# A smaller first mix, pooled outputs summed in PSUM, and the second phase in five chunks, in a kernel of attention, channel mix and gated convolution

## The chip, the cores and the metric

The kernel runs on one core of a Trainium2 chip. The metric is device time in microseconds (us) of one execution; three executions of the kernel before took 561.58, 561.82 and 563.68 us, a median of 561.82. TensorE (PE) multiplies, VectorE (DVE) and ScalarE (ACT) work elementwise, GpSimd (POOL) does small fills, and SyncE (SP) issues most of the DMA transfers. Each engine works through its own instructions in the order in which they were written; semaphores hold an instruction back until what it needs is there.

## The reference

Three layers follow each other. Layer 1, for 4 batches, 8 heads, 576 tokens and 64 channels a head, is the sum of an attention over tokens averaged in fours (repeated four times) and a local attention over the tokens nearer than 4. Its output has T = 2304 rows of 512 channels. Layer 2 mixes each row with the one before it, and layer 3 is a gated convolution.

```python
out_d = sm_attn(q_d, k_d, v_d)                  # means of 4 tokens
out_up = np.repeat(out_d, factor, axis=2)
mask = np.abs(pos[:, None] - pos[None, :]) < factor
...
x = out_up + out_local
...
xk = mu_k * x + (1.0 - mu_k) * x_prev
xr = mu_r * x + (1.0 - mu_r) * x_prev
k = np.maximum(xk @ w_k, 0.0)                   # 512 -> 1024
v = k * k @ w_v                                 # 1024 -> 512
r = 1.0 / (1.0 + np.exp(-(xr @ w_r)))           # 512 -> 512
x = r * v
...
h = np.maximum(x @ w_in, 0.0)                   # 512 -> 1024
conv_out += conv_w[k][None, None, :] * hp[:, k:k + S, :]   # 3 taps
gate = 1.0 / (1.0 + np.exp(-conv_out))
return h * gate @ w_out                         # 1024 -> 512
```

## The kernel before, in words

All of it is one program of steps. Every step names its engine, what it reads and what it writes; a long table of numbers (ORDER, line 24) gives the order in which the steps are emitted, and a second one (SECOND) says, where two engines could do a step, which does it. The order of each engine's instructions is thereby fixed by hand; nothing is reordered later. Channels lie on the partitions and tokens along the columns.

Phase one is the attention and the first matrix products (w_k and w_v). Attention goes by batch, by groups of four heads (two groups a batch) and by blocks of 32 tokens (18 blocks). For a group there are pooled keys and queries (a DVE sum of fours, line 511), local scores (PE, lines 540 and 549), their softmax on DVE and ACT, pooled scores (line 614), transposes (690, 741), pooled outputs (709, copied to the tile od by ACT, 721) and local outputs (760). A DVE add (775) sums the two into the tile xT. The matrix products are done by chunks of tokens (`chunks_`, line 258): 288, 288 and then 432 at a time. The first chunk is special: batch 0 is attended in two parts, blocks 0 to 9 and blocks 10 to 17 (`half`, line 432), and the first 288 tokens go through `first_mix` (line 851) while the second part and batch 1 are still being attended. There the weights arrive through three buffers st_d; two ACT instructions (382, 401) and one DVE instruction (385) turn each 512 KB tile into f32, and PE multiplies by the f32 tile as it stands, up (862) and down (892). The same tile is then split into a high part (ACT or DVE, 421/423) and a low part (DVE, 427) of a rounded type. All later chunks use three products of these parts (`mix`, line 916, with lines 926 and 976). Ten steps of idle products (`fills`, line 1032) keep PE occupied at the start.

The pooled values of batch 0 are made by PE from the value tile vw (`fold`, line 484). So the first output of a head group waits for its vw transfer.

Phase two goes over T in six chunks of 384 outputs (CH, line 247), each computed on 386 columns, as the convolution needs one neighbour on each side. For each chunk: `load_chunk` (1175) reads x back from DRAM and mixes rows, `gate` (1252) makes r and x1 (line 1259: 4 tiles of 12 products), `hidden` (1292) makes h (line 1303: 8 tiles of 12 products), the three taps (1348, 1349, 1352) and the gate, and `outp` (1375) multiplies by w_out, 24 products of 512 columns for 128 tokens (line 1383), one chunk late beside the next one. Here the two edge columns of each chunk are computed twice, once in either chunk.

## Time and profile before

| what | value |
|---|---|
| median of three runs | 561.82 us |
| the profiled execution's own time | 561.85 us |
| its span, first to last instruction | 560.0 us |
| PE busy | 545.9 us, 97% |
| DVE busy | 370.1 us, 66% |
| ACT busy | 306.6 us, 55% |
| mean granted TensorE clock | 0.990 |

The span is 1.85 us shorter than the profiled execution's time. Busy time is the share in which at least one instruction of the engine runs. The chain of waits follows the work that ended last back to its start; it names, for each stretch of time, the engine and line that the end hung on. The granted clock is the share of TensorE's full rate.

### The profile page before, as it was taken

The page shows a single profiled execution, that of the slowest core. Times are in us where ns is not written, and L with a number is a line of the kernel's source. Part 1 is how long each engine was busy: PE and PEld are TensorE (multiplying, and loading weights), DVE is VectorE, ACT ScalarE, POOL GpSimd, SP SyncE. Part 2 cuts the span into 40 slices and gives each one's busy share as a digit, 9 for nine tenths or more (in the row PEclk, how much of TensorE's full clock was granted, in tenths as well). Part 3 has the DMA queues.
Part 4 walks back from the last instruction along what each step waited for, and adds up shares of the span by engine and source line. Part 5 has one row for each costly group of instructions (what it writes and reads, how often), then busy time and mean ns, then how long its engine had stood idle before and what let it go on. Part 6 is the DMA issues. An engine that isn't in the chain of part 4 may idle for free.

```text
span 560.0 us, 12998 instructions
## 1 busy us (share of the span) xinstructions
PE 545.9 (97%) x5412; PEld 495.1 (88%) x5412; DVE 370.1 (66%) x720; ACT 306.6 (55%) x716; POOL 29.5 (5%) x132
## 2 busy tenths in 40 slices
PE   6899989999999999999999999999999999999996
PEld 3677769999999999999999998898998998999985
DVE  5778777677566646563374897487667676677750
ACT  4678956736553656554575555454545355444431
POOL 5001010110101000000000000000000000000000
PEclk9979998999999999999999999999999999999999
DMA  8658767647643503722127400402200130001002
GB/s 345 224 181 261 242 204 265 197 122 237 180 184 89 198 2 134 259 94 95 66 70 253 135 2 0 151 1 76 75 1 38 58 96 19 1 0 39 10 29 94
DMA packets 26395, 66.19 MB, mean 118 GB/s; under 512 B 2656, under 2 KB 12384, under 8 KB 25312
## 3 DMA queue, kind: packets, MB, share of 16 engines
q1 hardware_dynamic: 24608, 62.41, 31.7%
q0 software_dynamic: 1728, 2.95, 3.3%
q8 instruction: 42, 0.69, 0.5%
q14 instruction: 17, 0.14, 0.1%
HBM read 51.20 MB, written 14.16 MB: 117 GB/s over the span
## 4 chain that ended last, share of the span: by engine, by line
PE 93%; DMA 2%; DVE 2%; ACT 1%; issue 1%; SPq 0%; ACTq 0%; DVEq 0%
PE a L1383 18%; PE mm L926 16%; PE mm L976 16%; PE mm L1303 9%; PE a L1303 8%; PE a L1259 4%; PE mm L1259 4%; PE mm L862 3%; PE a L760 3%; PE mm L892 3%; DMA vw<-in_vw 2%; PE a L709 2%; PE a L549 2%; PE a L741 2%; PE a L690 1%; PE a L614 1%
## 5 line engine op out<-in xcount | busy, mean ns | idle before, releaser
L1383 PE MATMUL a<-wk,wv 128*128 128x512 f32 x432 | 101.0, 390 | 0.1
L1383 PEld LDWEIGHTS a<-wk,wv 128*128 128x128 f32 x432 | 80.9, 188 | 16.4 <-ACT xT L1398 0.4
L926 PE MATMUL mm<-xk,wk 128*128 128x432 f32 (+1 forms) x480 | 93.8, 353 | 0.0
L976 PE MATMUL mm<-k,wv 128*128 128x432 f32 (+1 forms) x480 | 91.1, 347 | 0.0
L926 PEld LDWEIGHTS mm<-xk,wk 128*128 128x128 f32 x480 | 85.8, 192 | 3.5 <-issue 0.5
L976 PEld LDWEIGHTS mm<-k,wv 128*128 128x128 f32 x480 | 84.9, 188 | 3.5 <-issue 0.4
L1303 PE MATMUL mm<-k,wi 128*128 128x386 f32 x288 | 53.9, 339 | 0.5 <-ACT k L1284 0.5
L1303 PE MATMUL a<-k,wi 128*128 128x386 f32 x288 | 54.0, 338 | 0.0
L1303 PEld LDWEIGHTS mm<-k,wi 128*128 128x128 f32 x288 | 51.0, 188 | 1.5 <-ACT k L1284 0.8
L1358 ACT ACTIVATE tmp<-tmp 128x384 f32<-128x384 f32 x48 | 25.0, 524 | 49.7 <-DVE tmp L1352 49.7
L1303 PEld LDWEIGHTS a<-k,wi 128*128 128x128 f32 x288 | 51.1, 188 | 0.5
L945 ACT ACTIVATE tmp<-mm 128x432 f32<-128x432 f32 (+1 forms) x40 | 20.2, 507 | 31.2 <-PE mm L926 21.6
L1361 DVE SCALAR_TENSOR_TENSOR tmp<-tmp,h 128x384 f32<-128x384 f32 x48 | 26.3, 556 | 10.0 <-ACT tmp L1358 8.5
L1370 DVE TENSOR_TENSOR wv<-tmp,wv 128x384 fp32r<-128x384 f32 x48 | 26.2, 554 | 8.5 <-ACT wv L1368 8.0
L1352 DVE SCALAR_TENSOR_TENSOR tmp<-h,cw_sb,tmp 128x384 f32<-128x384 f32 x48 | 29.7, 619 | 2.4
L1349 DVE SCALAR_TENSOR_TENSOR tmp<-h,cw_sb,tmp 128x384 f32<-128x384 f32 x48 | 29.7, 619 | 2.1
L1368 ACT CAST wv<-tmp 128x384 fp32r<-128x384 f32 x48 | 23.8, 509 | 13.0 <-DVE tmp L1361 13.0
L1348 DVE TENSOR_SCALAR tmp<-h,cw_sb 128x384 f32<-128x384 f32 x48 | 20.0, 418 | 15.3 <-ACT h L1333 7.8
L385 DVE SCALAR_TENSOR_TENSOR st_f<-st_f,st_d 128x512 uint32<-128x512 uint32 x28 | 19.2, 684 | 16.6 <-ACT st_d L401 16.6
L965 DVE TENSOR_TENSOR k<-tmp,k 128x432 fp32r<-128x432 f32 (+1 forms) x40 | 22.3, 575 | 8.9 <-ACT k L957 8.5
L910 ACT COPY tmp<-mm 128x432 f32<-128x432 f32 (+1 forms) x24 | 11.5, 481 | 30.3 <-PE mm L976 18.3
L1259 PE MATMUL a<-xk,wr 128*128 128x386 f32 x144 | 26.5, 338 | 0.0
(157 smaller groups left out, 813.9 us busy)
## 6 DMA issues: line engine op xcount, KB each, us to landing
vw<-in_vw SPq DMA_DIRECT2D x7, 1152.0 KB, 8.2
kq<-in_kq SPq DMA_DIRECT2D x6, 1152.0 KB, 6.5
x_d<-xT SPq DMA_DIRECT2D x16, 288.0 KB, 6.1
out_dram<-xT SPq DMA_DIRECT2D x18, 256.0 KB, 2.1
st_d<-in_moe_w_k SPq DMA_DIRECT2D x8, 512.0 KB, 4.4
st_d<-in_moe_w_v SPq DMA_DIRECT2D x8, 512.0 KB, 4.4
st_d<-in_moe_w_in SPq DMA_DIRECT2D x8, 512.0 KB, 4.7
st_d<-in_moe_w_out SPq DMA_DIRECT2D x8, 512.0 KB, 3.8
```

The source lines that it names most:

```text
L926: nc.tensor.matmul(pst[:, 0:n], lhsT=wk_t[wt][:, kt, mt * P:(mt + 1) * P], rhs=late["xk"][:, xs, kt, 0:n], start=(kt == 0 and g == 0), sto ...
L965: lambda e, r=r, j=j: e.tensor_sub(late["k2"][1][:, j, 0:n], r, late["k2"][0][:, j, 0:n].bitcast(F32)),
L976: nc.tensor.matmul(pst[:, 0:n], lhsT=wv_t[wt][:, kt, mt * P:(mt + 1) * P], rhs=late["k2"][xs][:, at[kt], 0:n], start=(kt == 0 and g == 0), ...
L1259: nc.tensor.matmul(pst[:, 0:CW], lhsT=late["wr"][wt][:, kt, mt * P:(mt + 1) * P], rhs=r_t(xs)[:, kt, :], start=(kt == 0 and g == 0), stop= ...
L1303: nc.tensor.matmul(pst[:, 0:CW], lhsT=late["wi"][wt][:, kt, mt * P:(mt + 1) * P], rhs=x1s(xs)[:, kt, :], start=(kt == 0 and g == 0), stop= ...
L1349: nc.vector.scalar_tensor_tensor(out=cv, in0=tap(0), scalar=cw[:, 0, mt:mt + 1], in1=cv, op0=ALU.mult, op1=ALU.add)
L1352: nc.vector.scalar_tensor_tensor(out=cv, in0=tap(2), scalar=cw[:, 2, mt:mt + 1], in1=cv, op0=ALU.mult, op1=ALU.add)
L1358: step("ACT", act(CH), lambda: nc.scalar.activation(cv, cv, AF.Tanh, scale=0.5), (), [cvk])
L1361: lambda: nc.vector.scalar_tensor_tensor(out=gt, in0=cv, scalar=1.0, in1=tap(1), op0=ALU.add, op1=ALU.mult),
L1368: step("ACT", act(CH), lambda: nc.scalar.copy(gh, gf), ["wv_old", gk], [("gh", j)])
L1370: ("DVE",), (0.56,), lambda e: e.tensor_sub(gl, gf, gh.bitcast(F32)),
L1383: nc.tensor.matmul(pst, lhsT=xs[:, tt * P:(tt + 1) * P], rhs=wo[wt][:, kt, :], start=(kt == 0 and g == 0), stop=(kt == KF - 1 and g == 2),)
```

## The change

1. `NH`, the first chunk, goes from 288 to 192 tokens, and chunk 1 from 288 to 384. Batch 0 is split after block 6 instead of block 10. The squares of the first mix get a tile of their own (sq) instead of batch 1's xT.
2. For the first part of batch 0 the pooled outputs are not copied to od and added by DVE. `down` multiplies the transposed pooled scores, each column read four times, into the PSUM tile of the local outputs, and the local products add to it; one copy (ACT or DVE) takes it to xT.
3. The inner loops of the local scores, the pooled scores and the local outputs change places: for scores the head runs outside and the parity r inside, for outputs the parity outside and the head j inside.
4. The fills of probs and of the picking tiles on POOL become steps of the order. The first key/query tile is loaded pair by pair, and at the start other transfers come first.
5. Phase two goes in five chunks of 384, 512, 512, 512 and 384 outputs. A chunk runs two columns ahead (`ahead`); the last three columns of h are copied by POOL to a tile edge and from there into the next chunk's h, so that no column is computed twice. Where a batch begins inside a chunk, a zero column is put in and ReLU and gate are done in two pieces. Odd chunks' v go to st_d, and so do the outputs' staging tiles.
6. ORDER and SECOND are new tables for the new steps. Two constants of the planner's costs (a product's fixed time, POOL's start) are changed; nothing at run time reads them.

```diff
-    0, 4, 80, 1, 88, 5, 96, 8, 64, 78, 11, 12, 10, 13, 62, 14, 66, 18, 79, 15, 69, 19, 25, 16, 20, 63, 24, 67,
...
-    NH = S // 2
+    NH = S // 3
...
-    chunks_ = [(0, NH), (NH, NH)] + [(t, NT) for t in range(S, B * S, NT)]
+    chunks_ = [(0, NH), (NH, S - NH)] + [(t, NT) for t in range(S, B * S, NT)]
...
-    CH = 384
-    NCH = T // CH
-    CW = CH + 2
+    CH = 512
+    ahead = 2
+    per = [3, 4, 4, 4, 3]
+    outs = [(P * sum(per[:i]), P * sum(per[:i + 1])) for i in range(len(per))]
...
+    spans = [(o0 + ahead * (o0 > 0), o1 + ahead * (o1 < T)) for o0, o1 in outs]
...
-    half = NB // 4 * 2 + 2
+    half = NB // 6 * 2
...
                 for e in range(ea, eb):
-                    for r in range(2):
-                        for h in range(4):
+                    for h in range(4):
+                        for r in range(2):
...
+                    def down(pr=pr, pst=pst, pdt=pdt, nq=nq, qs=qs):
+                        for c in range(nq):
+                            n_e = min(2, ne - 2 * c)
+                            for kc in range(2):
+                                for r in range(2):
+                                    for j in range(2):
...
+                                        nc.tensor.matmul(
...
+                                            lhsT=g["vd"][0][:, pr, kc, j * D:(j + 1) * D],
+                                            rhs=z.unsqueeze(3).to_broadcast([HC, n_e, PB, FAC]),
+                                            start=(c == 0 and kc == 0), stop=False,
+                                        )
...
                     for e in range(ne):
-                        for j in range(2):
-                            for r in range(2):
-                                k = slice(64 * r, 64 * r + W)
+                        for r in range(2):
+                            k = slice(64 * r, 64 * r + W)
+                            for j in range(2):
...
+                if over:
+                    xv = x[:, hp, 1 + t0:1 + t0 + nt].rearrange("p (e r s) -> p r e s", r=2, s=BQ)
+
+                    def cp(e, pst=pst, xv=xv):
...
+                    step(("ACT", "DVE"), (act(nt), 0.12 + 1.0e-3 * nt), cp, (), [(pk, 0), (pk, 1)] + ks, slack=SL[0])
+                    continue
...
-        squares = xT[1].rearrange("p a s -> p (a s)")[:, 0:KF * NH].rearrange("p (k s) -> p k s", k=KF)
-        over = [("xT", 1, x, c) for x in range(KM) for c in (0, half)]
+        squares = [sq_t[:, i] for i in range(KF - 2)] + [tmp[:, 4 + i % 2, 0:NH] for i in range(KF - 2, KF)]
...
         def pad():
             h = late["h"][i]
-            at = {0: 0, 1: HCH + 1, 2: CW - 1}[kind]
-            nc.gpsimd.memset(h[:, at:at + 1], 0.0)
-
-        step("POOL", 0.11, pad, ["late"], [(hk, "pad")])
+            if c:
+                nc.gpsimd.tensor_copy(h[:, 0:lead], late["edge"][0][:, mt])
+            else:
+                nc.gpsimd.memset(h[:, 0:1], 0.0)
+            for t in seam:
+                nc.gpsimd.memset(h[:, lead + t - a:lead + t - a + 1], 0.0)
...
+        if e < T:
+            step(
+                "POOL", 0.12,
+                lambda: nc.gpsimd.tensor_copy(late["edge"][0][:, mt], late["h"][i][:, end - ahead - 1:end]),
+                ["late", (hk, "d")], [("edge", mt)],
+            )
```

The new lines of the rows below: 383 and 409 are the loads of lines 369 and 395, 555, 564, 629 and 805 are the PE lines 540, 549, 614 and 760, 919 is 862, and `down` is 786; on DVE 833, 888, 902, 646 and 647 are 775, 831, 845, 631 and 632.

The transfers that SP issues first, before the change (kq and kq_f are keys and queries of batch 0's two head groups, vw and vw_f their values, st_d the weights' buffers):

```order
L369 DMA kq_126<-in_kq 128x2x896
L369 DMA kq_f_127<-in_kq 128x2x896
L395 DMA st_d_110<-in_moe_w_k 128x1024
L369 DMA vw_130<-in_vw 128x2304
L395 DMA st_d_111<-in_moe_w_k 128x1024
L369 DMA vw_f_131<-in_vw 128x2304
L395 DMA st_d_112<-in_moe_w_k 128x1024
```

And after it:

```order
L383 DMA kq_126<-in_kq 128x768 x2
L383 DMA kq_126<-in_kq 128x2x384
L383 DMA kq_f_127<-in_kq 128x768 x2
L383 DMA vw_130<-in_vw 128x2304
L383 DMA vw_f_131<-in_vw 128x2304
L409 DMA st_d_110<-in_moe_w_k 128x1024
L1062 DMA mus<-in_mu 128x8
```

Both value tiles now stand ahead of the first weights, and the first keys and queries come in smaller pieces.

PE just before its first product of the first mix, before the change (a_ are PSUM tiles of the attention, mm_ those of the mix):

```order
L760 MATMUL a_178<-pt_136,vw_f_131 64x32 x20
L760 MATMUL a_179<-pt_136,vw_f_131 64x32 x20
L540 LDWEIGHTS ident_71
L540 MATMUL a_178<-mask,ident_71 128x152
L540 LDWEIGHTS ident_71
L540 MATMUL a_178<-mask,ident_71 128x114
L540 LDWEIGHTS ident_71
L540 MATMUL a_178<-mask,ident_71 128x38
L549 MATMUL a_178<-kq_126 32x38 x16
L614 MATMUL a_179<-kqd_128 32x144 x8
L549 MATMUL a_178<-kq_126 32x38 x16
L862 MATMUL mm_174<-tmp,st_f_113 128x288 x4
```

And after it:

```order
L786 MATMUL a_158<-pdt_139,vd_f_133 64x32 x8
L805 MATMUL a_157<-pt_136,vw_f_131 64x32 x12
L805 MATMUL a_158<-pt_136,vw_f_131 64x32 x12
L555 LDWEIGHTS ident_71
L555 MATMUL a_157<-mask,ident_71 128x228
L555 LDWEIGHTS ident_71
L555 MATMUL a_157<-mask,ident_71 128x190
L555 LDWEIGHTS ident_71
L555 MATMUL a_157<-mask,ident_71 128x38
L564 MATMUL a_157<-kq_126 32x38 x48
L629 MATMUL a_158<-kqd_128 32x144 x12
L919 MATMUL mm_154<-tmp,st_f_114 128x192 x4
```

The local outputs that end the first part are shorter (12 products instead of 20), the new products of `down` stand ahead of them, and the scores of the second part, which stand before the first mix in both, are longer.

DVE at the end of the first mix, before the change, from the pooled sums of the next group to the maxima of the pooled scores of batch 1's second group:

```order
L511 TENSOR_REDUCE kqd_128<-kq_126 128x288
L845 TENSOR_TENSOR xk<-tmp,xk 128x288 x2
L775 TENSOR_TENSOR xT_120<-a_179,od_140 128x9x32 x2
L831 SCALAR_TENSOR_TENSOR tmp<-xT_119,mus,tmp 128x288
L775 TENSOR_TENSOR xT_120<-a_178,od_140 128x9x32 x2
L845 TENSOR_TENSOR xk<-tmp,xk 128x288
L831 SCALAR_TENSOR_TENSOR tmp<-xT_119,mus,tmp 128x288
L427 TENSOR_TENSOR wv_118<-st_f_113,wv_117 128x4x128
L845 TENSOR_TENSOR xk<-tmp,xk 128x288
L631 TENSOR_REDUCE sums_145<-a_178 128x3
```

And after it:

```order
L888 SCALAR_TENSOR_TENSOR tmp<-xT_119,mus,tmp 128x384
L833 TENSOR_TENSOR xT_120<-a_158,od_140 128x9x32 x2
L902 TENSOR_TENSOR xk<-tmp,xk 128x384 x2
L833 TENSOR_TENSOR xT_120<-a_157,od_140 128x9x32 x2
L888 SCALAR_TENSOR_TENSOR tmp<-xT_119,mus,tmp 128x384 x2
L902 TENSOR_TENSOR xk<-tmp,xk 128x384 x2
L646 TENSOR_REDUCE sums_145<-a_157 128x3
```

The same work of batch 1 stands ahead of the low parts xk of chunk 1 in both, with 384 columns in place of 288.

## Rows read from the trace of the kernel before

**Rows 1.** The page's first part: busy us (share) x instructions.

```profile
PE 545.9 (97%) x5412; PEld 495.1 (88%) x5412; DVE 370.1 (66%) x720; ACT 306.6 (55%) x716; POOL 29.5 (5%) x132
```

**Rows 2.** Busy time by engine in four stretches, with clock and DMA.

```profile
core 0: us, PE busy (x) PEld busy (x) DVE busy (x) ACT busy (x) POOL busy (x), PEclk, DMA share, GB/s
0.00:29.45 29.45, 22.28 (x568) 14.91 (x568) 19.38 (x49) 17.84 (x49) 8.21 (x41) 0.96 0.71 271
29.45:82.00 52.55, 52.50 (x931) 40.25 (x932) 40.72 (x86) 42.16 (x104) 4.31 (x7) 0.96 0.74 235
84.00:303.26 219.26, 219.22 (x2608) 206.60 (x2609) 132.84 (x249) 124.31 (x290) 10.59 (x21) 0.99 0.47 152
303.26:560.00 256.74, 251.59 (x1296) 233.05 (x1295) 175.95 (x334) 121.47 (x272) 5.61 (x63) 1.00 0.14 49
```

**Rows 3.** The chain that ended last, start and length in us: start, first mix.

```profile
2.30 10.71 DMA vw<-in_vw
13.15 1.92 PE mm L484 x17
...
29.45 6.17 PE mm L862 x16
...
38.95 0.62 PE a L709 x16
...
68.26 1.30 PE a L709 x16
...
73.10 1.18 PE a L760 x72
74.28 4.08 PE mm L892 x16
...
79.97 0.80 PE a L549 x64
...
82.00 1.68 issue
83.96 4.90 PE mm L926 x24
...
89.95 1.58 PE mm L926 x12
```

**Rows 4.** The same chain, later: products of 432, 386, 512 columns, last outputs.

```profile
228.06 18.80 PE mm L926 x96
...
303.26 4.24 PE mm L1259 x24
...
332.94 5.47 PE a L1383 x24
...
539.09 16.36 PE a L1383 x72
```

**Rows 5.** Busy time by engine in four short stretches, columns as in group 2.

```profile
10.00:12.00 2.00, 2.00 (x89) 1.39 (x74) 1.93 (x6) 1.99 (x8) 0.49 (x3) 1.00 1.00 407
28.00:30.00 2.00, 1.95 (x81) 1.55 (x63) 1.83 (x8) 1.94 (x4) 0.00 (x0) 0.50 0.01 4
85.00:86.00 1.00, 1.00 (x6) 1.00 (x6) 0.96 (x3) 0.30 (x2) 0.00 (x0) 0.50 0.88 138
450.00:456.00 6.00, 6.00 (x34) 5.85 (x33) 5.43 (x11) 3.30 (x8) 0.00 (x0) 1.00 0.58 159
```

**Rows 6.** DVE by line and shape: busy us, mean ns, idle before.

```profile
L511 DVE TENSOR_REDUCE kqd<-kq 128x288 f32<-128x1152 f32 x12 | 16.1, 1346 | 1.6 <-DMA kq<-in_kq 1.6
...
L775 DVE TENSOR_TENSOR xT<-a,od 128x288 f32<-128x288 f32 x24 | 9.7, 451 | 6.1 <-PE a L760 6.1
...
L581 DVE TENSOR_REDUCE sums<-probs 128x18 f32<-128x702 f32 x6 | 5.3, 882 | 3.5 <-ACT probs L578 3.5
L566 DVE TENSOR_TENSOR probs<-a,sums 128x684 f32<-128x684 f32 x6 | 5.2, 872 | 0.2
...
L423 DVE CAST wk<-st_f 128x512 fp32r<-128x512 f32 x5 | 2.1, 424 | 0.1
```

More of the change, by code (lines that the diff above doesn't have):

```diff
@@ L138 @@
     OVER = {"DVE": 0.083, "ACT": 0.105, "PE": 0.165, "POOL": 0.07}
-    BEGIN = {"DVE": 0.9, "ACT": 3.8, "PE": 3.9, "POOL": 6.0, "SP": 0.7, "GQ": 6.0}
+    BEGIN = {"DVE": 0.9, "ACT": 3.8, "PE": 3.9, "POOL": 3.4, "SP": 0.7, "GQ": 6.0}
     def __init__(self, on):
@@ L452, in loads @@
             tag("lk", i0)
-            load(
-                t[:, :, a:e], kq[b, 2 * gp:2 * gp + 2, :, a:e].rearrange("r p s -> p r s"), 2 * (e - a), (),
-                [(k, i0)] + ([(k, half)] if whole else []), SL[i0 > 0],
-            )
+            for prs in ((0,), (1,)) if b == 0 and i0 == 0 else ((0, 1),):
+                p0, p1 = prs[0], prs[-1] + 1
+                load(
+                    t[:, p0:p1, a:e], kq[b, 2 * gp + p0:2 * gp + p1, :, a:e].rearrange("r p s -> p r s"),
+                    len(prs) * (e - a), (),
+                    [(k, i, pr) for pr in prs for i in ({0, half} if whole else {i0})], SL[i0 > 0],
+                )
             if i0:
@@ L748, in local_out @@
                 step("ACT", act((e - a) * P), cp, (), pks + [(ptk, a)], slack=SL[i0 > 0])
-            od, odk = g["od", i0]
+            over = b == 0 and i0 == 0
+            if not over:
+                od, odk = g["od", i0]
             x = xT[b % 2]
@@ L898, in down @@
                     step(
-                        "PE", us, f, [wk] + [("sq", kt) for kt in range(a, a + 4)] + over, [pk], due=due(us, PACE)
+                        "PE", us, f, [wk] + [sqk[kt] for kt in range(a, a + 4)], [pk], due=due(us, PACE)
                     )
@@ L1215, in load_chunk, with get @@
-        ch["v"] = (vi, ("v", vi))
-        first = [t - lo + 1 for t in range(0, T, S) if lo - 1 <= t <= hi]
+        t0s = [t for t, m in chunks_ if t < e and t + m > a]
+        for i in range(2 if vi else 1):
+            def get(i=i):
+                k0, k1, t = v_dst(vi)[i]
+                nc.sync.dma_start(out=t[:, :, 0:n], in_=v_d[k0:k1, :, a:e].rearrange("k p s -> p k s"))
+            k0, k1 = (2 * i, 2 * i + 2) if vi else (0, KM)
+            step(
+                "SP", dma_us((k1 - k0) * n), get,
+                [v_old[vi]] + [("v_d", t, mt) for t in t0s for mt in range(KM)],
+                [("v", vi, kt) for kt in range(k0, k1)],
+            )
@@ L1293, in hidden @@
         prog.tag = "h", c
-        kind = c % 3
         pst, pk = ring("mm2", mm2)
+        a, e = spans[c]
+        n, m = e - a, outs[c][1] - outs[c][0]
+        seam = seams[c]
+        lead = ahead + 1 if c else 1
         old = [("mm", pk[1]) if pk[1] < 2 else "a1_old"]
@@ new lines, in hidden @@
+        step("ACT", act(n) + 0.15 * gap, relu, ["late"], [pk, (hk, "d")])
+        if e < T:
+            step(
+                "POOL", 0.12,
+                lambda: nc.gpsimd.tensor_copy(late["edge"][0][:, mt], late["h"][i][:, end - ahead - 1:end]),
+                ["late", (hk, "d")], [("edge", mt)],
+            )
+        def tap(o):
+            return late["h"][i][:, o:o + m + gap]
+        parts = [0] + [t - outs[c][0] for t in seam] + [m]
+        cv, cvk = ring("cv", cv_t)
+        gt, gk = ring("gt", gt_t)
@@ L1347, in conv @@
+        cv, gf = cv[:, 0:m + gap], gt[:, 0:m]
         def conv():
@@ L1388, in outp @@
             us = 12 * pe(DM) + TAIL
-            js = [gts[c, kt][2] for kt in range(a, a + 4)]
+            js = [gts[c, kt] for kt in range(a, a + 4)]
             step(
@@ L1408, in tile_local_attention__then__channel_mix__then__conv_glu @@
         main_ += [lambda mt=mt: hidden(c, mt) for mt in range(GB - KF)]
-        side = [lambda tt=tt: outp(c - 1, tt) for tt in range(CH // P)] if c else []
+        side = [lambda tt=tt: outp(c - 1, tt) for tt in range(per[c - 1])] if c else []
         done = 0
@@ L1419, in tile_local_attention__then__channel_mix__then__conv_glu @@
             hidden(c, mt)
-    for tt in range(CH // P):
+    for tt in range(per[-1]):
         outp(NCH - 1, tt)
```

295 lines of the change are left out of this document (162 added, 133 removed), and 169 rows, old and new, of tables (ORDER, SECOND).

## The prediction

> **What bounds the kernel now.** I read the page's busy shares first: PE is busy 97% of the span, DVE 66%, ACT 55% [rows 1]. The stretches by stage then say where PE is not the bound [rows 2]. From 84 us on it is busy to within 0.04 us up to 303 us, and in phase two up to the last output at 539.09 + 16.36 = 555.45 us [rows 2, 4]. There only PE's own work counts. Before 29.45 us it is busy 22.28 of 29.45 us, part of that with fills, and the chain runs through a transfer: vw, issued at 2.30 us, takes 10.71 us, and only then fold starts at 13.15 us [rows 2, 3]. In the first mix, 29.45 to 82.00 us, PE is full again, with DVE at 40.72 and ACT at 42.16 of 52.55 us [rows 2]. At 82.00 us PE stands for 1.68 us without a wait that the profile names ("issue"), and the clock falls to half after it [rows 3, 5].
>
> So I ask for every edit what it does to PE's work, and for the first mix, where DVE's reserve is smallest, what it does to DVE.
>
> **The start.** Ahead of vw stood 896 + 896 + 512 KB; now stand 3 x 384 + 768 KB, 384 KB less. At the 407 GB/s of 10 to 12 us [rows 5] that is 1 us: fold at about 12.1. From fold to the first product of the mix passed 29.45 - 13.15 = 16.3 us [rows 3]. Now change:
> - `down`, per head group, issues 32 records of 64 columns and 32 of 32 columns. Line 709 took 0.62 us for 16 records of 64 columns and 1.30 us for 16 of 160 [rows 3], 39 and 81 ns, so about 25 ns at 32 columns: 32 x 39 + 32 x 25 ns = 2.0 us. The old line 709 at 96 columns, on that line 0.85 us, goes: +1.2 us a group, +2.4 us.
> - Local outputs of 4 fewer blocks a group: a record takes 1.18 us / 72 = 16 ns [rows 3], 64 records fewer: -1.0 us.
> - The second group's scores now stand behind fold: estimated +1.3 us from the same record times.
> - Waits go: the od copies, the last DVE add, and mixing on 192 instead of 288 columns. By bounds: 0 if PE hides them, 2.5 us if all stand in the chain; I take 1.5.
>
> Sum 12.1 + 16.3 + 2.4 - 1.0 + 1.3 - 1.5 = 29.6 us less the fills and gaps behind fold, some 2 us: 27.5 us. Ends 25.5 and 30.
>
> **The first mix.** Its 128 records of 288 columns take 4.08 us per 16 [rows 3], 32.6 us; the first 16 took 6.17, so 34.7 us with the half clock, which the row at 28 to 30 us shows as 0.50 [rows 3, 5]. That leaves 52.55 - 34.7 = 17.9 us of attention. With 192 columns the products take two thirds, 22 us. The second part of batch 0 grows from 8 to 12 blocks in each of two groups, 8 block shares; the stretch held about 40 (16, a whole group of 18, a third of another), so 17.9 x 8/40 = +3.6 us. PE needs 22 + 17.9 + 3.6 = 43.5 us and would be done at 71.0 us.
>
> DVE does not shrink with it. Its weight work is the same 16 tiles. Eight more block shares cost 0.5 us each: a group of 18 has two pooled sums of 1.35 us, four instructions of about 0.87 us on scores and probabilities, four adds of 0.45 us [rows 6], 8.0 us, and small ones of about 1 us, over 18. That is +4.0 us. DVE does three more casts to the high part here, 0.42 us each [rows 6], +1.3 us. So 40.72 + 4.0 + 1.3 = 46.0 us [rows 2]. Nothing behind the low parts xk can start earlier, as the order shows, and chunk 1 needs them. DVE's share in this stretch was 77.5%; where the chain ran through DVE, at 450 to 456 us, it held 90.5%; at 28 to 30 us 91.5%, at 10 to 12 us 96.5% [rows 2, 5]. I take 93%, nearest to the stretches in which it is pushed: 49.5 us. Chunk 1 starts at 27.5 + 49.5 = 77.0 us instead of 83.96; the ends are 71.0 (PE paces) and, at 77.5%, 59.4 us, 86.9. ACT loses columns and keeps some 40 us in 49.5. DMA must move 235 GB/s x 52.55 us = 12.3 MB in 49.5 us, 250 GB/s, against 407 reached [rows 2, 5].
>
> **The stop at 82 us.** It came where 72 output records and a group's scores stood together; now eight mix products stand between. I take it as gone; its 1.68 us is in the 83.96. After it 24 products took 4.90 us where 2 x 1.58 = 3.16 is normal, at clock 0.50 [rows 3, 5]: -1.7 us. Ends: -1.7 and, if it comes again elsewhere, +1.7.
>
> **Chunk 1** goes from 288 to 384 columns. Twelve products take 1.58 us at 288 [rows 3] and 18.80/8 = 2.35 us at 432 [rows 4]; 384 lies two thirds between, 2.09. Sixteen tiles: 16 x 0.51 = +8.2 us, all on PE.
>
> **Phase two.** 864 products of 386 columns at 4.24/24 = 0.1767 us are 152.6 us. Now 432 of 512 columns at 5.47/24 = 0.2279 [rows 4], 98.5 us, and 288 of 386 and 382 columns, 50.7: 149.2, -3.5 us. The output products stay. DVE has 69% of this stretch [rows 2] and its work per column stays; POOL's edge copies (its whole load is 29.5 us [rows 1]) stand ahead of the taps like the fills that they replace. If each of four seams waits 1 us, +4; cost taken: none.
>
> **Loop order** (edit 3). No row shows the new sequence. Below: at most the 0.80 us / 64 = 12.5 ns of line 549 [rows 3], 3.9 ns less on 1152 records of local outputs (eight groups of 144), -4.5 us. Above: 25 ns as in line 709, where neighbouring products share their rows [rows 3], 9 ns x 1152 = +10 us. I take 0: tiles still follow each other on different places of the array. The Trainium skill ("TensorE: Matmul & The Clock Gate", "Part 3: Packing small matmuls — row/col tiling") says that a weight load overlaps running products only when the row group differs; the new order repeats the row group. By the rule these products slow down, and the sum becomes rival 3's; line 709 shows such neighbours overlapping at least in part, since 160 columns cost 81 ns, so the trace does not settle it.
>
> **Sum.** Against the profiled execution's 561.85 us (the median is 561.82): (77.0 - 83.96) - 1.7 + 8.2 - 3.5 = -4.0, 557.8 us. The last chunk again has three output tiles, so the tail is the same.
>
> **Rivals.**
> 1. PE paces the first mix too. For it: PE's order is full of mix products, and DVE reached 96.5% in places. Against: 46.0 us of DVE work in 43.5. Chunk 1 at 71.0: 551.8 us.
> 2. DVE keeps its present 77.5% since it waits for ACT's cuts between weight tiles. Place: first mix; chunk 1 at 86.9; 567.7 us, slower. It decides from a share of 86% down, where chunk 1 starts at 81.0 and the gain is used up. Against: in the stretch before, DVE waited because PE set the pace.
> 3. Repeated row groups slow the small products, up to +10 us: 567.8. From 4 ns a record on, the gain is gone.
> 4. The five chunks don't do what they should: seams wait 1 us each, 561.8, no change.
>
> **How the numbers follow.** Forecast, DVE-paced first mix between 88 and 97%: 0.47, own range 555 to 560.5. Rival 1: 0.19. Rival 2: 0.14. Rival 3: 0.08. Rival 4: 0.12. A measurement can tell 0.5% (2.8 us) from no change, so faster means below 559.0: 0.37 of the forecast's 0.47, all of rival 1, in sum 0.56. Slower, above 564.6: three quarters of rivals 2 and 3, 0.16. No change: the rest, 0.28. The range is 550.5 to 564.5: rival 1 with a start at 26 us below, and above it two thirds of rivals 2 and 3 left out.
>
> **What would show it.** First mix starting near 27.5 us and chunk 1 near 77 us; DVE above 88% between them and PE with waits for st_f, tmp or xk there; no stop without a name; 12 products of chunk 1 in 2.1 us; 2.73 us for 12 products of 512 columns in gate and hidden; phase two about 3.5 us shorter from its first gate to the last output; local outputs at 16 ns a record. It would be wrong if chunk 1 started after 81 us, if local outputs took 20 ns, or if PE waited for edge or h at the seams.

## The result, and the profile after

The changed kernel took 556.18 us, the median of four executions (555.21 to 557.57), where the kernel before took 562.59 us on the same chip. The ratio is 0.9888, with a 95% interval of 0.9854 to 0.9921: 1.1% faster. The forecast was 557.8 us. Twelve more executions at a later time, told below (run 9), gave 0.9927 [0.9900, 0.9954]. So the medians differ by 4.5 and by 6.4 us.

The profiled execution took 556.9 us, its span is 554.8 us, and its granted clock is 0.995. The page's busy shares, to be held against [rows 1]:

```profile
PE 538.7 (97%) x5364; PEld 479.4 (86%) x5364; DVE 366.3 (66%) x689; ACT 300.3 (54%) x676; POOL 43.5 (8%) x181
```

PE has 7.2 us less to do, and no engine that waits for it has more than before, except POOL with its edge copies. The stretches, now from the first product of the first mix to chunk 1, from there to phase two, and phase two up to its last output [rows 2]:

```profile
28.25:76.95 48.70, 44.51 (x1057) 40.03 (x1054) 44.74 (x91) 38.89 (x100) 4.17 (x5) 0.98 0.77 257
76.95:304.12 227.17, 226.37 (x2616) 212.11 (x2609) 136.15 (x256) 128.34 (x296) 11.20 (x21) 1.00 0.47 148
...
304.12:550.48 246.36, 246.34 (x1152) 212.25 (x1151) 169.68 (x304) 116.24 (x239) 19.94 (x113) 1.00 0.15 49
```

PE stays 4.2 us short of full in the first mix, where before it was short by 0.05. In phase two it is full. The PE timeline shows the places behind these sums (start, busy length, what ran, and in brackets the idle time ahead of it with its releaser):

```profile
11.96 1.92 PE L499 MATMUL mm<-vw,tmp 128*32 128x256 f32 x18 [1.29 <-DMA vw<-in_vw]
...
17.59 2.06 PE L786 MATMUL a<-pdt,vd 80*64 80x64 f32 x64
...
25.41 0.37 PE L555 MATMUL a<-mask,ident 128*128 128x228 bf16 x3 [0.81 <-ACT xT L822]
...
28.25 2.52 PE L919 MATMUL mm<-tmp,st_f 128*128 128x192 f32 x8
...
76.95 3.41 PE L983 MATMUL mm<-xk,wk 128*128 128x384 f32 x18
80.85 5.37 PE L983 MATMUL mm<-xk,wk 128*128 128x384 f32 x30 [0.49 <-issue]
```

Fold starts at 11.96 us, the mix at 28.25, chunk 1 at 76.95. The stop without a name [rows 3] is there again, 0.49 us long, now 18 products into chunk 1. Two shorter ones, of 0.31 us each, end at 26.63 and 100.47 us. The chain of waits gives the products' rates:

```profile
87.31 2.11 PE mm L983 x12
...
95.99 2.23 PE a L805 x144
...
304.12 4.23 PE mm L1324 x24
...
457.41 2.72 PE a L1467 x12
...
484.61 4.16 PE mm L1324 x24
...
523.26 27.22 PE a L1467 x120
```

Twelve products of 384 columns take 2.11 us, 12 of 512 columns 2.72, 24 of 382 columns 4.16. Phase two starts at 304.12 us where it started at 303.26 [rows 4], and it lasts 246.36 us where it lasted 252.19. So chunk 1 starts 7.0 us earlier, its greater width and what remains of the stop give back all of that and 0.86 us more, and the whole gain is made in phase two.

### The profile page after: what moved, and what is told of

Same layout as the page of the kernel before. It is cut to its first block, busy times and chain, and to the rows that moved or that the text cites. A ratio compares the mean times of both kernels' runs of the same rounds, so it can differ in the third digit from the quotient of the medians.

```text
span 554.8 us, 12885 instructions
## 1 busy us (share of the span) xinstructions
PE 538.7 (97%) x5364; PEld 479.4 (86%) x5364; DVE 366.3 (66%) x689; ACT 300.3 (54%) x676; POOL 43.5 (8%) x181
## 4 chain that ended last, share of the span: by engine, by line
PE 91%; DMA 3%; DVE 3%; ACT 1%; issue 1%; SPq 0%; ACTq 0%; DVEq 0%
PE a L1467 18%; PE mm L983 17%; PE mm L1033 17%; PE mm L1372 9%; PE a L1372 9%; PE mm L1324 4%; PE a L1324 4%; PE a L805 3%; PE mm L919 2%; DMA st_d<-in_moe_w_v 2%; DMA vw<-in_vw 2%; PE a L703 1%; PE a L727 1%; PE a L564 1%; PE a L759 1%; PE a L629 1%
## 5 line engine op out<-in xcount | busy, mean ns | idle before, releaser
L1033 PE MATMUL mm<-k,wv 128*128 128x432 f32 (+1 forms) x480 | 95.6, 356 | 0.0
L1467 PE MATMUL a<-wk,wv 128*128 128x512 f32 x342 | 81.0, 389 | 0.0
L1467 PEld LDWEIGHTS a<-wk,wv 128*128 128x128 f32 x342 | 64.2, 188 | 13.3
L1372 PE MATMUL mm<-k,wi 128*128 128x512 f32 (+2 forms) x240 | 52.0, 368 | 0.0
L1372 PE MATMUL a<-k,wi 128*128 128x512 f32 (+2 forms) x240 | 51.9, 368 | 0.0
L1439 ACT ACTIVATE tmp<-tmp 128x513 f32<-128x513 f32 (+1 forms) x40 | 23.6, 592 | 36.3 <-DVE tmp L1433 36.1
L1442 DVE SCALAR_TENSOR_TENSOR tmp<-tmp,h 128x384 f32<-128x384 f32 (+3 forms) x64 | 26.9, 456 | 7.2 <-ACT tmp L1439 5.8
L1433 DVE SCALAR_TENSOR_TENSOR tmp<-h,cw_sb,tmp 128x513 f32<-128x513 f32 (+1 forms) x40 | 28.0, 700 | 1.8
L1430 DVE SCALAR_TENSOR_TENSOR tmp<-h,cw_sb,tmp 128x513 f32<-128x513 f32 (+1 forms) x40 | 28.0, 700 | 1.8
L1453 DVE TENSOR_TENSOR wv<-tmp,wv 128x512 fp32r<-128x512 f32 (+1 forms) x32 | 20.0, 628 | 11.6 <-ACT wv L1451 11.4
L1429 DVE TENSOR_SCALAR tmp<-h,cw_sb 128x513 f32<-128x513 f32 (+1 forms) x40 | 18.4, 460 | 12.2 <-ACT h L1409 11.3
L1451 ACT CAST wv<-tmp 128x512 fp32r<-128x512 f32 (+1 forms) x32 | 17.9, 571 | 11.8 <-DVE tmp L1442 11.6
```

The costliest lines, as they stand in the source:

```text
L1033: nc.tensor.matmul(pst[:, 0:n], lhsT=wv_t[wt][:, kt, mt * P:(mt + 1) * P], rhs=late["k2"][xs][:, at[kt], 0:n], start=(kt == 0 and g == 0), ...
L1372: nc.tensor.matmul(pst[:, 0:n], lhsT=late["wi"][wt][:, kt, mt * P:(mt + 1) * P], rhs=x1s(xs, kt)[:, 0:n], start=(kt == 0 and g == 0), stop ...
L1430: nc.vector.scalar_tensor_tensor(out=cv, in0=tap(0), scalar=cw[:, 0, mt:mt + 1], in1=cv, op0=ALU.mult, op1=ALU.add)
L1433: nc.vector.scalar_tensor_tensor(out=cv, in0=tap(2), scalar=cw[:, 2, mt:mt + 1], in1=cv, op0=ALU.mult, op1=ALU.add)
L1439: step("ACT", act(m), lambda: nc.scalar.activation(cv, cv, AF.Tanh, scale=0.5), (), [cvk])
L1442: nc.vector.scalar_tensor_tensor(out=gf[:, o:q], in0=cv[:, o + j:q + j], scalar=1.0, in1=tap(1)[:, o + j:q + j], op0=ALU.add, op1=ALU.mult,)
```

## The experiments

The kernel before ran beside them, with medians of 562.03 us (runs 1 to 4), 560.48 (5 to 8), 561.77 (9 to 11) and 562.13 (12); each ratio is to the runs on its own chip.

**1. The old loop order.** The changed kernel with the loops of its small products as they were.

```diff
-                    for h in range(4):
-                        for r in range(2):
+                    for r in range(2):
+                        for h in range(4):
...
-                        for r in range(2):
-                            k = slice(64 * r, 64 * r + W)
-                            for j in range(2):
+                        for j in range(2):
+                            for r in range(2):
+                                k = slice(64 * r, 64 * r + W)
```

> The changed kernel with edit 3 alone undone: local scores, pooled scores and local outputs loop over r and j in the order of the kernel before; the order of steps is that of the changed kernel. My theory (the order of these loops costs nothing): same time as the changed kernel, 556.2 +- 1 us; local outputs 2.23 us per 144 records, as in both kernels. Rival (the new order repeats the row group and slows its records, and something else pays for it): faster than the changed kernel by up to 10 us; local outputs below 2.1 us per 144.

Measured: 557.57 us, ratio 0.9934 [0.9900, 0.9969]. The local outputs, 1008 of them, are busy for 16.5 us with either order. Its PE timeline shows what else this execution had:

```profile
76.73 3.39 PE L983 MATMUL mm<-xk,wk 128*128 128x384 f32 x18
83.80 6.98 PE L983 MATMUL mm<-xk,wk 128*128 128x384 f32 x30 [3.69 <-issue]
```

The stop comes after the same 18 products, but is 3.69 us long, and the 30 products behind it take 6.98 us instead of 5.37. The loops neither cost nor give anything that these runs can tell; the longer stop and the slower products make 4.8 us, all of the 4.2 us between the two profiled executions (561.14 and 556.9 us).

**2. Five chunks alone.** The kernel before with phase two of the changed kernel; phase one is as it was. The order of the steps was joined from the two tables.

```diff
-    CH = 384
-    NCH = T // CH
-    CW = CH + 2
+    CH = 512
+    ahead = 2
+    per = [3, 4, 4, 4, 3]
```

> The kernel before with one part of the change: phase two in five chunks with carried edge columns. Start, first mix and the steps up to phase two stand as in the kernel before; the steps of phase two stand as in the changed kernel. My theory (the gain is that of phase two, and the first mix on 192 columns gives back in chunk 1 what it gains): phase two takes about 246.4 us from its first gate to its last output, against 252.2, and the kernel 562.6 - 6 = 556.6 us, ratio to the kernel before 0.989; the stop at 82 us and the half clock behind it stay. Rival (the first mix is where the change gains, phase two only the 3.5 us of the forecast): 559.1 us, ratio 0.994. Second rival (the five chunks need the memory or the order of the changed first part): no gain, 562 us.

Measured: 561.55 us, 1.0000 [0.9972, 1.0028]. Phase two lasted 246.67 us, 5.5 less than before, nearly as in the changed kernel. But ahead of it stood PE waits that the joined order itself made, and a stop:

```profile
PE a L551 <- issue: 2.3, 1, 2.3
PE mm L978 <- ACT tmp L912: 1.9, 1, 1.9
```

(Engine and line, what it waited for, us in total, times, longest.) The run shows the gain in phase two, and does not yet say what the edits alone are worth.

**3. Less DVE work.** The pooled sums of the first mix read one token of four.

```diff
+            few = 1 if b == 1 or i0 else FAC
...
-                        d[:, a // FAC:e // FAC], t[:, a:e].rearrange("p (s t) -> p s t", t=FAC), axis=AX.X
+                        d[:, a // FAC:e // FAC], t[:, a:e].rearrange("p (s t) -> p s t", t=FAC)[:, :, 0:few],
+                        axis=AX.X
```

> The changed kernel, with less for DVE in the first mix: the pooled sums of batch 0's second part and of batch 1 read one token of four (three quarters of these sums are left out), four instructions of 1.34 us in the first mix, about 0.4 us each when a quarter is read: DVE has 3.8 us less between 28 and 77 us. Theory 1 (DVE paces the first mix): chunk 1 starts 3 to 3.8 us earlier than at 76.95 us, 73.2 to 74 us, and the time falls to about 552.8 us. Theory 2 (the w_v tiles pace it, since DMA is full from 48 to 68 us): chunk 1 starts at most 1 us earlier, time 555.2 to 556.2.

Measured: 557.31 us, 0.9912 [0.9885, 0.9939]. DVE's work in the first mix falls by 2.9 us, the stretch by 0.7:

```profile
28.32:76.33 48.01, 44.61 (x1058) 39.76 (x1055) 41.81 (x91) 38.90 (x99) 4.17 (x5) 0.98 0.77 256
```

If DVE had set the pace, the stretch would have followed it. It hardly does.

**4. Less traffic.** The second batch's keys, queries and values are loaded in part, an eighth and a ninth of the columns.

```diff
+                e1 = a + (e - a) // 8 if b == 1 else e
...
+            n = NB // 2 * 4 * D // (9 if b == 1 else 1)
```

> The changed kernel, with less for DMA in the first mix: batch 1's loads of kq and vw are cut to an eighth and a ninth of their columns (the rest of the tiles keeps batch 0's values), so that of some 12.6 MB between 28 and 77 us about 3 MB go. Theory 1 (DVE paces): the waits of ACT for w_v tiles (3.2 us) go, but chunk 1 starts at most 0.8 us earlier, which is DVE's own wait for kq; time 555.4 to 556.2. Theory 2 (the w_v tiles pace it): the last w_v tile lands 4.8 instead of 9.6 us after its issue, chunk 1 starts 2.5 to 4 us earlier than at 76.95 us, and the time falls to 552.2 to 553.7.

Measured: 555.03 us, 0.9880 [0.9820, 0.9940].

```profile
27.62:75.10 47.48, 43.92 (x1058) 39.09 (x1055) 45.37 (x93) 39.59 (x101) 4.17 (x5) 1.00 0.64 187
```

The first mix takes 47.48 us, 1.2 less, with DVE at 95.6% of it. Half of that is PE's own work, 43.92 us instead of 44.51: the mean clock of the stretch is 1.00 here and 0.98 in the changed kernel's execution. So 0.6 us is what less traffic can have given in the first mix. Chunk 1's first 48 products ran through in 8.88 us with no stop.

**5. Five chunks again.** As in 2, but from the first product of chunk 2 on the order is that of the changed kernel.

> Once more the kernel before with phase two in five chunks alone. In the first try phase two itself took 246.67 us instead of 252.19, but the order in which I had joined the two lists made PE wait 2.9 us for ACT ahead of phase two. Now the steps up to the first product of batch 2's mix stand as in the kernel before, and all later ones as in the changed kernel. My theory (the gain is phase two's): no waits of PE between its chunk 1 and phase two, phase two 246.4 us, and the kernel 5.8 us faster than before, ratio 0.9895. Rival (the first part of the change gains too): phase two as said, but the changed kernel stays 2 us or more ahead of this one.

Measured: 566.97 us, 1.0096 [1.0073, 1.0118], slower than before, with every execution between 564.7 and 567.5. Its PE timeline has four stops, none with a named wait:

```profile
84.46 0.29 PE L551 MATMUL a<-kq 64*32 64x38 f32 x11 [2.44 <-issue]
...
131.61 0.59 PE L551 MATMUL a<-kq 64*32 64x38 f32 x42 [1.67 <-issue]
...
165.32 0.27 PE L551 MATMUL a<-kq 64*32 64x38 f32 x6 [1.47 <-issue]
...
190.87 3.79 PE L978 MATMUL mm<-k,wv 128*128 128x432 f32 x11 [2.78 <-issue]
```

They sum to 8.4 us. Three of them stand within or at the end of a group's scores, dense rows of small products, and the fourth one product behind such a row. The first stands 11 scores ahead of chunk 1; in run 2, whose program is the same up to there, it stood at the same product. The kernels of runs 1 and 3 and the changed kernel, whose PE programs have equally many products up to there, all stopped behind the 18th product of chunk 1. So the place belongs to the program, and the length differs from one trace to the next.

What it is can be seen in the trace of transfers. PE's program itself comes by a queue of its own. From the changed kernel's page, the whole execution (packets, MB, share of 16 engines):

```profile
q8 instruction: 42, 0.69, 0.5%
```

That is 16 KB a packet, and 5364 products and 5364 weight loads make 10,728 instructions, 255 a packet, so about 128 products with their loads. The products from one of run 5's stops to the next, in the windows' PE column, are just such pieces, 7, 4 and 3 of them:

```profile
84.46:131.61 47.15, 45.44 (x896) 41.98 (x895) 33.59 (x64) 28.60 (x82) 4.84 (x6) 0.96 0.66 206
131.61:165.32 33.71, 32.25 (x511) 29.17 (x511) 18.40 (x35) 16.87 (x42) 2.41 (x3) 0.95 0.40 113
165.32:190.87 25.55, 22.77 (x383) 20.56 (x384) 14.72 (x26) 12.83 (x34) 1.60 (x2) 1.00 0.57 182
```

One such packet, from the changed kernel's trace, among the transfers that began between 78.00 and 79.00 us:

```profile
q8 instruction: 1, 0.02, 5.6%
```

It took 5.6% of what 16 engines have in 1 us, 0.9 us. The packet before the stop began at 78.4 us in the changed kernel, and PE went on at 80.85; in run 1 at 81.2 and 83.80; in run 3 at 78.8 and 81.14; in the kernel before at 81.4 and 83.67. In run 5 three began at 129.3, 162.9 and 188.5, and PE went on at 131.61, 165.32 and 190.87. Each time PE goes on 2.2 to 2.6 us behind the packet's beginning (in run 2, where it took 1.75 us, 3.1), and 1.3 to 1.6 us behind its end, run 2 included. (The expectation of run 6, below, says that packets land 2.3 to 2.6 us before PE goes on; these are their beginnings.) In run 4 the packet began at 74.8, early enough, and there was no stop. I formed the theory: PE's code comes in pieces, the dense small products use up a piece of 128 in about 2 us (144 local outputs take 2.23), and where the packet with the next has not ended 1.3 us ahead of its use, PE stands.

The Trainium skill ("Runtime: NRT & Kernel Launch", "Instruction fetch mechanics") says that each engine's program is refilled in blocks of 16 KiB, 256 instructions, by a DMA queue of its sequencer, and that crossing a border is mostly hidden. The size agrees with the 42 packets. Most borders do pass without a stop here, but not all: a kernel has none to four stops of 0.3 us or more, the longest 3.69 us.

**6. Fewer transfers around that packet.** In the changed kernel, two weight tiles of w_r and a key/query tile are issued later by SP, past chunk 1's start.

```
-L409 DMA st_d_112<-in_moe_w_r 128x1024
-L409 DMA st_d_111<-in_moe_w_r 128x1024
 L383 DMA vw_130<-in_vw 128x2304
-L383 DMA kq_126<-in_kq 128x2x1152
...
+L383 DMA kq_126<-in_kq 128x2x1152
 L383 DMA vd_132<-in_vp 80x512
+L409 DMA st_d_112<-in_moe_w_r 128x1024
+L409 DMA st_d_111<-in_moe_w_r 128x1024
```

> The changed kernel with three loads moved on SP's queue, nothing else: the two w_r tiles of 66.7 us behind the vd load of batch 2 (about 91 us), and batch 2's kq load of 77.06 us behind the last store of the first mix's outputs (about 79.7 us). Theory (the stop at the start of chunk 1 is PE waiting for its next code: a 16 KB packet of the instruction queue lands 2.3 to 2.6 us before PE goes on in every trace, and it lands late when the data queues are full): that packet lands at 77.7 us or earlier, the stop (0.49, 1.5 and 3.69 us in the traces of the changed kernel and its two variants) and the half clock behind it are gone, and the median falls by 0.5 to 2 us against the changed kernel's, with less spread. Rival (the stop has to do with the block of small products alone): stop of 0.5 us or more again at the same place.

Measured: 557.77 us, 0.9948 [0.9926, 0.9969]. The packet began at 75.9, and chunk 1's first 48 products ran in 8.89 us without a stop. What was won there was lost behind it:

```profile
99.38 0.51 PE L983 MATMUL mm<-xk,wk 128*128 128x384 f32 x2 [0.84 <-issue]
119.75 2.30 PE L805 MATMUL a<-pt,vw 38*64 38x32 f32 x144 [0.70 <-DMA vw<-in_vw]
```

Another piece came late, and a value tile, late in turn, made PE wait 0.70 us; the clock fell to a mean of 0.79 between 122 and 130 us. Phase two started at 305.35, no earlier than in the changed kernel.

**7. The tiles of w_v sooner.** As 6, with the last tiles of w_v loaded and cut earlier and two of DVE's casts given to ACT. On ACT, for example:

```
+L435 CAST wv_117<-st_ff_146 128x4x128
+L435 CAST wv_117<-st_ff_147 128x4x128
+L396 ACTIVATE st_ff_147<-st_d_110 128x512
+L415 ACTIVATE st_d_110<-st_d_110 128x512
```

> The kernel of the run before this one, and three more moves in the first mix: batch 1's second kq load goes behind the last w_v tile instead of ahead of it, its two pooled sums stand behind the parts of that tile on DVE, and two casts of w_v parts go from DVE to ACT, which waits there for w_v tiles. Theory (from 54 to 68 us the w_v tiles pace the first mix, then DVE up to chunk 1): ACT's waits for w_v tiles fall from 3.2 us to below 1.5 us, DVE's idle 1.8 us between 64 and 68 us goes, and chunk 1 starts 1.5 to 2.5 us earlier than at 76.95 us; the time falls to 552.5 to 554.5 us. Rival (DMA has to bring the same bytes by then, so something waits as long): chunk 1 at 76.5 us or later.

Measured: 560.03 us, 0.9987 [0.9962, 1.0011]: the gain is gone. PE waited four times between 59 and 68 us, for DVE and ACT, which had been given work ahead of the softmax, and then the clock stayed low, as the timeline and the stretch from 70 to 78 us show:

```profile
61.09 1.26 PE L703 MATMUL a<-ident,pd 128*80 128x128 f32 x10 [1.40 <-DVE pd L673]
...
67.89 0.33 PE L759 MATMUL a<-ident,probs 128*128 128x128 f32 x1 [0.93 <-ACT pt L764]
...
70.42 4.07 PE L805 MATMUL a<-pt,vw 38*64 38x32 f32 x144
```

```profile
70.00:78.00 8.00, 8.00 (x157) 7.51 (x156) 6.77 (x13) 3.71 (x9) 1.94 (x3) 0.50 0.51 133
```

144 local outputs took 4.07 us instead of 2.30, and chunk 1 started at 81.78 us. So an order that PE waits for a little can cost twice: the waits and then the 1.2 GHz level. A stop of 1.42 us without a name followed at 104.3 us.

**8. Less of both.** Runs 3 and 4 together.

> The changed kernel with both cuts at once: the pooled sums of e3 (a quarter of the tokens read) and the loads of e4 (an eighth of kq, a ninth of vw of batch 1). Alone they brought chunk 1 0.6 and 1.85 us forward. Theory (DMA and DVE pace the first mix in turn, so each alone uncovers the other): together more than the sum of 2.4 us, chunk 1 at 72.5 to 74 us, where PE's own work (44.5 us behind 28.2) takes over at 72.8. Rival (something third, the chains of softmax steps through PE, DVE and ACT, sets the pace): no more than the sum, chunk 1 at 74.5 us or later.

Measured: 556.26 us, 0.9918 [0.9894, 0.9941].

```profile
29.16:76.56 47.40, 43.82 (x1057) 39.10 (x1054) 42.35 (x93) 39.63 (x101) 4.16 (x5) 1.00 0.63 188
```

The first mix takes 47.40 us with DVE at 42.35, no more than 0.1 shorter than in run 4. So neither DVE nor the transfers hold it there, singly or together. PE's own work is 43.82 us, and 3.6 us of its idle time remain. (This execution lost about 1 us at the start: fold waited 1.7 us for its tile and took 3.60 us instead of 1.92.) PE's waits in this stretch, in us:

```profile
PE a L707 <- DVE pd L677: 1.4, 1, 1.4
PE a L731 <- ACT pdt L713: 0.9, 1, 0.9
PE a L633 <- ACT pd L660: 0.7, 1, 0.7
PE a L559 <- DVE probs L585: 0.5, 1, 0.5
```

All four are for single steps of the softmax (probs, pd) or for the copy of its transposed result (pdt), and they sum to 3.5 us. In the changed kernel's own trace most of the 4.2 us are such waits too. That the first mix would shorten by as much without them is read from the traces and was not tested.

**9. The changed kernel again.** No edit; twelve executions.

> The changed kernel once more, unchanged, as the yardstick for the runs beside it. In the first comparison it took 556.18 us (4 runs), ratio 0.9888. If the stop of PE at the start of chunk 1 differs from one execution to the next (0.49, 1.5 and 3.69 us in three traces with the same work there), single runs spread over 3 us or more and a second trace shows another length of the stop than 0.49 us; if it belongs to the program alone, the trace shows 0.4 to 0.6 us again.

Measured: 557.31 us (555.67 to 561.23), 0.9927 [0.9900, 0.9954]. In its profile chunk 1 runs through:

```profile
76.88 8.60 PE L983 MATMUL mm<-xk,wk 128*128 128x384 f32 x48
```

```profile
76.88:302.90 226.02, 226.02 (x2616) 212.03 (x2609) 135.17 (x254) 128.42 (x295) 11.18 (x21) 1.00 0.46 148
```

The same program stopped for 0.49 us in one execution and not at all in another, where the packet began at 77.4 us instead of 78.4. The stop is therefore part of this kernel's spread, 555.7 to 561.2 us.

**10. All of w_r later.** The four tiles of w_r are loaded, and so cut, later than in run 6. On SP:

```
-L409 DMA st_d_112<-in_moe_w_r 128x1024
-L409 DMA st_d_111<-in_moe_w_r 128x1024
...
-L409 DMA st_d_110<-in_moe_w_r 128x1024
...
+L409 DMA st_d_112<-in_moe_w_r 128x1024
+L409 DMA st_d_111<-in_moe_w_r 128x1024
+L409 DMA st_d_110<-in_moe_w_r 128x1024
```

> The changed kernel with loads moved out of the way of PE's code: the w_r tiles, which nothing needs before phase two, from 66.7, 106 and 124 us behind batch 3's first loads (from about 143 us on), with the instructions that cut them moved along, and batch 2's first kq load behind the last store of the first mix as in e6. Theory (PE's code waits behind data; e6 lost its gain again because the w_r tiles then stood ahead of the code at 97 us and of vw at 106 us): chunk 1 at 75.4 us without a stop, no stop above 0.3 us up to phase two, phase two from 301.5 to 302.5 us, and a time 1.5 to 2.5 us below the changed kernel beside it. Rival (the queues are as full without them, or DVE is late with the moved cuts): same time as the changed kernel within 1 us, with a stop or wait of PE elsewhere.

Measured: 561.80 us, 1.0002 [0.9973, 1.0030]. No stop up to 150 us, but then PE waits for ACT, and ACT for DVE, on which the moved cuts stand in a heap:

```profile
169.61 0.66 PE L759 MATMUL a<-ident,probs 128*128 128x128 f32 x4 [2.51 <-ACT pdt L709]
```

```profile
161.76 1.64 ACT L671 ACTIVATE pd<-pd,sums 128x144 f32<-128x144 f32 x5 [3.76 <-DVE sums L536]
...
166.89 0.67 ACT L396 ACTIVATE st_f<-st_d 128x512 f32<-128x512 f32 x1 [1.80 <-DVE wr L441]
```

Moving these transfers and their cuts to spare the packet thus cost more than the stop.

**11. Five chunks alone, joined late.** As 5, but the two orders meet at the first product of the fifth chunk of phase one (chunk 4); all ahead of it is the order of the kernel before.

> Third try of the kernel before with phase two in five chunks alone. Now the order of the kernel before holds up to the first product of batch 3's second chunk (about 228 us), with all its loads, and only what follows stands as in the changed kernel. Theory (phase two gains 5.5 to 5.8 us wherever it stands; the two tries lost it again to waits for ACT and to four stops of 8.4 us in a stretch whose loads I had moved): no stops but that at 82 to 84 us, phase two 246.6 us, the kernel 4.5 to 6 us faster than before, ratio 0.989 to 0.992. Rival (the five chunks cost something ahead of phase two, whatever the order): again no gain, ratio 0.996 or more.

Measured: 556.96 us, 0.9912 [0.9878, 0.9946], beside 557.31 of run 9 on the same chip.

```profile
83.53 0.29 PE L551 MATMUL a<-kq 64*32 64x38 f32 x11 [1.84 <-issue]
83.75 4.97 PE L928 MATMUL mm<-xk,wk 128*128 128x288 f32 x24
```

Phase two lasts 246.38 us. The kernel keeps the old first mix, has the stop at 81.7 us and the slow products behind it, 4.97 us for 24, and is as fast as the changed kernel. So the five chunks in this order give the whole gain, and what the rearranged first mix nets cannot be told from nothing with 5 and 12 executions. Phase two is as short in every trace with five chunks, 246.4 to 246.7 us, also in runs 2 and 5, where the order of the rest lost the gain.

**12. The code's borders moved.** Run 11's kernel with its early fills cut into narrow products, the same columns in all, which shifts every border between two pieces of PE's program.

```diff
-            for _ in range(2):
+            for n in [1] * 10 + [3] * 2:
                 nc.tensor.matmul(
-                    mm_t[1][:, 0:8 * W], lhsT=ident16, rhs=mask[:, 1:2, :].to_broadcast([P, 8, W]),
+                    mm_t[1][:, 0:n * W], lhsT=ident16, rhs=mask[:, 1:2, :].to_broadcast([P, n, W]),
                     start=True, stop=True,
                 )
```

> The kernel with the five chunks alone (cut late), with nothing moved but the program's text: each fill ahead of fold and of the first mix is cut from two products of 304 columns into twelve narrow ones (ten of 38 columns and two of 114), the same columns in all. That is 100 product records and as many weight loads more, ahead of everything else, so each border between two 16 KB pieces of PE's program (128 products and their loads) lies 100 records earlier in the program, or, counted to the next border, 28 records later. Theory (the dense small products outrun the fetch of the program): in the run before, the stop of 1.84 us stood 11 records ahead of chunk 1, so the border moves to about the 17th product of chunk 1; these take 0.13 us each, which gives the piece over 2 us more to land, while it is asked for at most 0.5 us later. No stop of over 0.5 us between 80 and 84 us, chunk 1's first 24 products in 3.2 us instead of 4.97, phase two from about 300 us on, and 553.0 to 555.0 us where that kernel took 556.96, about 0.986 of the time before. Rival one: the piece comes late whatever stands ahead of it (the queues are full at that time): a stop of 1.5 to 2.5 us at 82 to 86 us, now inside chunk 1, half clock behind it, 556 to 558 us. Rival two: other borders now fall into other dense stretches and give a stop and a half clock elsewhere: the stop at 82 us gone, but one of 1 to 3 us at another place, 556 to 559 us.

Measured: 559.85 us, 0.9967 [0.9936, 0.9998].

```profile
12.13 0.76 PE L1034 MATMUL mm<-mask,ident 128*128 128x38 bf16 x19 [1.03 <-issue]
...
18.61 0.53 PE L1034 MATMUL mm<-mask,ident 128*128 128x38 bf16 x12 [0.88 <-issue]
...
83.25 3.42 PE L928 MATMUL mm<-xk,wk 128*128 128x288 f32 x24
...
151.85 0.72 PE L551 MATMUL a<-kq 64*32 64x38 f32 x58 [1.80 <-issue]
```

The stop at 82 us is gone, and chunk 1's first 24 products take 3.42 us. In its place are stops at 11.1, 17.7 and 150.1 us, which ended 2.4 us behind the beginnings of packets, at 9.7, 16.2 and 149.5. From the first to the second lie 128 products, one piece, and from there to the third 2555, 20 pieces less 5:

```profile
12.13:18.61 6.48, 5.60 (x128) 3.85 (x128) 4.31 (x11) 4.09 (x10) 0.00 (x0) 1.00 1.01 385
18.61:151.85 133.24, 126.60 (x2555) 106.60 (x2555) 99.21 (x204) 90.77 (x239) 12.35 (x16) 0.99 0.65 204
```

The theory on the place holds: the stops move with the borders, as rival two said. But they are not all of the time. Behind chunk 1's first products PE now waits 1.04 us for DVE and 1.55 us for a transfer, which it does not in run 11:

```profile
87.71 1.26 PE L692 MATMUL a<-ident,pd 128*80 128x128 f32 x10 [1.04 <-DVE pd L660]
...
92.10 1.31 PE L711 MATMUL a<-pdt,vd 80*64 80x160 f32 x16 [1.55 <-DMA vd<-in_vp]
```

So, as far as these two traces show, the stop at 82 us had covered part of what other engines were late with. I found no version with all of the work that beats both kernels.

## Why the prediction was right, and where it was not

**The sum.** Forecast 557.8 us, measured 556.18: the direction was right, and the size to 1.6 us, which is in part luck, as two errors went against each other. Up to phase two the forecast had -0.5 us, and the two profiled executions show +0.86; phase two had -3.5, and they show -5.8. The terms one by one:

- **The start.** Fold at 12.1 forecast, 11.96 measured; `down` 2.0 us, measured 2.06; the first mix at 27.5, measured 28.25. I had not counted PE's 0.81 us wait for the copy to xT, nor a stop of 0.31 us behind it.
- **The first mix.** 49.5 us forecast, 48.70 measured, chunk 1 at 77.0 and 76.95. DVE's share came out at 91.9% (93% taken), its work at 44.74 us (46.0). The number stands on a cause that holds only in part: I said that DVE sets the pace, so that DVE's work over its share gives the time. With 2.9 us of it gone the stretch lost 0.7 (run 3), and with traffic gone too, 1.3 (run 8), of which 0.7 is PE's own work at a higher clock. PE's work, 44.5 us (43.5 forecast), and its waits for single steps of the softmax make up the stretch. That 93% fitted is luck as much as reading. Rival 1 (PE alone paces) and rival 2 (DVE stays at 77.5%) are both refuted by the first window above.
- **The stop.** This is the step that failed as a cause. I took the stop as gone since eight mix products now stood between the small ones. They did not remove it: it moved behind 18 products of chunk 1, and its length goes from nothing (run 9) over 0.49 to 3.69 us (run 1). In the profiled execution it happened to be short, and so the term of -3.4 us, stop and slow products, looked right to 0.5 us. The kernel before varies as well: of its 88 executions beside the runs, the 33 with a granted clock of 0.995 or more have a median of 560.0 us, the 37 with less than 0.9915 one of 562.7. The forecast began from a trace of the second kind (561.85 us, 0.990); no trace of the first kind is kept, so how much of the -3.4 us belongs to that one execution stays open.
- **Chunk 1.** Twelve products of 384 columns 2.09 us forecast, 2.11 measured. In run 9, without a stop, chunk 1 to phase two lasted 226.02 us; before it was 219.30, of which 1.74 went with the slow products [rows 3]: +8.5 against the forecast +8.2.
- **Phase two.** -3.5 us forecast, -5.8 measured: the mis-sized term. Twelve products of 512 columns take 2.72 us (2.73 taken), and 382 columns are cheaper than 386, 0.1733 us (0.1767 taken); together the 720 products take 148.3 us instead of the 149.2 forecast, 4.3 less than the 152.6 that the prediction had for the 864 before. The other 1.5 us were small losses of the kernel before in this phase, which I had not read as such: a wait, and slow products behind it and near 461 us. The timeline of the kernel before:

```profile
355.05 3.75 PE L1303 MATMUL mm<-k,wi 128*128 128x386 f32 x18 [0.46 <-ACT k L1284]
...
461.55 3.02 PE L1383 MATMUL a<-wk,wv 128*128 128x512 f32 x12
```

  Eighteen products of 386 columns take 3.34 us in such a row of the changed kernel's timeline, and twelve of 512 columns 2.91 in the other rows of this one. The new phase two has no such place, and no seam made PE wait: 246.34 of 246.36 us are busy. Rival 4 is refuted.
- **Loop order.** 0 forecast, 0 measured: 2.23 us for 144 local outputs, 15.5 ns each, with the new order, and 1008 of them the same 16.5 us in all with the old (run 1); 1008 local scores take 12.2 us with the new order and 12.1 with the old. Rival 3 is refuted. By the rule of the Trainium skill ("TensorE: Matmul & The Clock Gate", "Part 3: Packing small matmuls — row/col tiling"), that a weight load overlaps only products of another row group, the new order should have been slower; these rows do not agree.

Taken together, the forecast's own net of the first-mix edits, -0.5 us, agrees with run 11, where leaving them out changed nothing that the runs can tell.

## What to carry to other kernels

Add up an edit that moves work between chunks to its end before calling it a gain: the first mix ended 7 us earlier and chunk 1 took it all back. Computing fewer columns twice on the engine that is full shortened phase two by 1% of the kernel's time in every trace, but two of three orders of the rest lost it again (runs 2 and 5). Where PE stands with no wait named, look for its program's packets just before it, and compare several executions and kernels by the product at which it stands before blaming the work around it.
